# Last batch's end: the last gated product in two token sets, every output tile its own transfer, the last tile in two column halves, and the order of the end drawn anew

## The chip, the cores and the metric

The kernel runs on one core of one Trainium2 chip. The core has a matrix engine (PE in the profile, with its weight loads as PEld), a vector engine (DVE), a scalar engine (ACT), GpSimd (POOL), and SyncE (SP), which here only issues transfers; 16 DMA engines move data between memory and the core. The metric is device time in microseconds, the median of several runs. "About 1%" is what a measurement of it can tell from no change.

## The reference

Clustered attention (4 batches, 8 heads, 768 tokens, head size 64: a query sees only keys whose nearest of 16 centroids is its own), and on its output a gated long convolution.

```python
def _moe_ref(x, w_proj, filter_fft, w_out):      # x: (4, 768, 512), the attention's output
    proj = x @ w_proj
    x1, x2, x3 = (proj[..., :D], proj[..., D:2 * D], proj[..., 2 * D:])
    X2 = np.fft.rfft(x2, n=S, axis=1)
    H = np.fft.rfft(filter_fft, n=S, axis=0)[None, :, :]
    x2_conv = np.fft.irfft(X2 * H, n=S, axis=1)
    y = x1 * x2_conv * x3
    return (y @ w_out).astype(np.float32)
```

All inputs and the output are float32; the output is 4 x 768 x 512.

## The kernel before

`build` makes a plan: a list of operations, each with the engines that could do it, a duration, what it reads and writes, and a due time. `Plan.follow` then lays the operations out in an order written by hand into the string `ORDER`. A word such as `P1543:2` is operation 1543 on PE with its result in PSUM bank 2; V is DVE, A is ACT, G is POOL, S is the SP queue. Each engine does its words from left to right. There are eight PSUM banks (0 to 7; 4 and 5 serve as one pair while attention runs), so a word that takes a bank waits until the last reader of that bank's former content is done.

`attention(n, pr)` does two head pairs at a time, `hyena(b)` does the convolution of batch b. The convolution of batch 2 and the attention of batch 3 are woven together; after them comes the convolution of batch 3, the last, with the rest of batch 2's.

The operations that matter here, by number (up to 1941 the same before and after):

- 1806, 1814, 1822, 1830: the last products of probabilities and values. 1831: the last accumulation of probabilities (L691). 1833: their sum over keys (L704, the denominator), 1834 its copy, 1835 a transpose, 1836 the reciprocal (V), 1837 and 1838 ("bc") spread it over the partitions, 1839 to 1842 multiply and write `xT`, the convolution's input (L772). 1781 and 1782 do the same for the pair before, with `rb`, which S1779 and S1780 load.
- 1843 to 1865: batch 3's projection x2 (1843/1844, 1846/1847, 1850/1851, 1853/1854 each in three quarters, which don't need the last pair, and one; 1857 and 1859 whole), the copies 1845, 1852, 1858, sums and differences on DVE (1848, 1849, 1855, 1856, 1860, 1861) and four sums `uv` (1862 to 1865, L467). 1866 to 1889: the spectrum, times the filter (L833), subtracted or added into `y` (L837: 1872, 1873, 1880, 1881, 1888, 1889).
- For each of four channel blocks dt: projections for x3 and x1 (two halves ch of 384 tokens each, 8 matmuls of 384 columns), a copy of x3 and the gate x1*x3 on DVE (L875), the inverse transform (1899, 1912, 1925, 1938, on two banks), a copy of one bank (1900, 1913, 1926, 1939), two folds (L910, batch 2 also L900), and the gated product `y2[:, dt]` (L913: 1903, 1916, 1929, 1942). For dt = 3: 1930, 1932 (ch 0), 1934, 1936 (ch 1), gates 1933 and 1937, folds 1940 and 1941.
- 1943 to 1964 before: the output. Six tiles of 128 tokens (index 2*tt + e_), each a product over four blocks with `w_out`, three quarters first (needing 1903, 1916, 1929) and one last quarter (needing 1942), then a copy (DVE or ACT) and a transfer on SP: tiles 0 and 1 together (524 KB), 2 and 3 together, 4 and 5 each alone (262 KB).
- Of batch 2: 1496 a projection and 1497 its gate; 1504, 1505, 1519, 1520, 1534, 1535, 1549, 1550 (L900) and 1506, 1507, 1521, 1522, 1536, 1537, 1551, 1552 (L910) its folds; 1508, 1523, 1538, 1553 its gated products; 1524 to 1547 its projections and inverse transforms (1517, 1532, 1547), with the copies 1533, 1544, 1548; 1554, 1556, 1559, 1561, 1564, 1566 its six output tiles, 1560 one of their copies. S1110 is the last 524 KB of batch 1's output.

An operation with `lock=True` on POOL waits for the locked DVE operation ahead of it in the order (L1175 to L1180); DVE doesn't wait for POOL in that way.

PE's products run as pairs of matmuls over 64 columns of weights each (`product`, L65); a product of eight matmuls is one output tile of 128 rows.

Of the kernel before, what the change touches and what calls it, by code (L numbers as in the profile page):

```python
# [23 lines left out]
NT = S // 128  # L24
# [190 lines left out]
A1817 A1811 P1103:1 P1108:3 A1109 P1496:2 V1721 S1779 A1890 S1780 P1502:60 A1503 V1815 V1823 A1104 P1806 P1517:31  # L215
V1505 S1105 A1827 P1511:7 V1831 P1814 P1822 V1504 A1518 P1830 V1512 A1832 V1507 V1506 V1519 V1520 P1833:6 A1834
P1532:07 P1835:6 P1528:5 V1836 P1837:6 V1781 P1838:3 V1782 P1843:1 P1853:4 V1839 V1840 V1841 V1842 P1844 V1497 V1508
P1857:3 A1858 V1522 V1521 G1523 A1533 V1535 P1846:2 V1534 G1536 G1537 A1845 P1847 P1850:6 P1851 V1849 V1848 A1852
P1854 P1859:1 V1860 V1861 P1908:7 A1909 P1547:30 A1529 V1855 V1863 P1539:2 G1862 P1541:7 V1856 G1865 G1864 V1548 V1549
P1524:5 A1525 P1526:1 V1527 A1540 V1542 P1530:6 P1910:2 V1911 V1531 G1538 P1545:5 P1921:1 V1550 G1551 P1866:2 V1867  # L220
P1543:6 A1544 P1869:3 V1868 V1871 V1870 V1546 P1917:0 P1906:2 V1552 A1922 V1553 P1934:1 A1935 P1936:3 V1937 G1872
A1918 P1904:5 G1873 P1919:0 V1920 P1874:1 V1875 P1885:3 P1877:6 P1893:0 V1878 P1556:7 G1880 V1876 V1879 P1882:4 V1883
V1886 A1905 S1110 P1891:5 A1892 G1881 V1884 P1559:1 G1888 P1554:5 P1923:6 P1561:4 A1555 A1557 V1887 V1889 P1895:7
A1896 V1907 V1560 A1562 V1894 P1912:53 V1913 V1914 V1915 P1897:1 V1898 P1899:04 A1900 V1924 S1558 P1564:5 A1565 V1902
P1566:1 A1567 V1901 V1903 P1925:36 A1926 V1916 P1930:1 A1931 P1938:04 S1563 V1927 P1932:1 V1928 V1929 P1957:6 S1568
A1939 V1941 V1940 V1933 V1942 P1953:3 P1950:4 P1943:1 P1958 V1959 S1960 P1951 A1952 P1954 A1955 S1956 P1944 P1946:0
P1947 V1945 A1948 S1949 P1961:4 P1962 A1963 S1964
# [3 lines left out]
def build(T):  # L231
# [548 lines left out]
    def hyena(b):  # L780
# [63 lines left out]
        for dt in range(ND):  # L844
# [58 lines left out]
            for s_, o_ in ((0, Alu.add), (1, Alu.subtract)):  # L903
# [9 lines left out]
            op(("DVE", .95) if last else {"DVE": .95, "POOL": 1.85}, lambda e, dt=dt, x3=x3, yy=yy: alu(e).tensor_tensor(  # L913
                T.y2[:, dt], yy().rearrange("p t c -> p (t c)"), x3().rearrange("p a b -> p (a b)"),
                op=Alu.mult), due + 2.5, r=ykeys + xkeys[0] + xkeys[1], w=[("y2", dt)], lock=True)
        for tt in range(3):
            ob, obk = (T_("tm", 0), [("tm", 0, 0), ("tm", 0, 1), ("tm", 0)]) if last and tt == 2 else (
                T_("ob", tt % 2), [("ob", tt % 2, 0), ("ob", tt % 2, 1), ("ob", tt % 2)])
            for e_ in range(2):
                h = Bank()  # L920
                due = step(.87)

                def W(e, kts=range(ND), tt=tt, e_=e_, h=h):
                    for kt in kts:
                        columns(ap(h), T.y2[:, kt, ts(2 * tt + e_, 128)], T.wout[:, kt], kt == 0, kt == ND - 1)
                if last:
                    op(("PE", .647), lambda e, W=W: W(e, range(3)), due, r=[("y2", dt) for dt in range(3)] + ["wout"],
                       w=[h], alloc=h, kind="proj")
                    op(("PE", .217), lambda e, W=W: W(e, range(3, 4)), due, r=[("y2", 3), h], w=[h], kind="proj")
                else:  # L930
                    op(("PE", .862), W, due, r=[("y2", dt) for dt in range(ND)] + ["wout"], w=[h], alloc=h,
                       kind="proj")
                op(EV512, lambda e, e_=e_, ob=ob, h=h: copy(e, ob()[:, e_], ap(h)), due + 1, r=[h],
                   w=[obk[e_], obk[2]], free=[h])
                if last and tt == 2:
                    op(("SP", .6), lambda e, tt=tt, e_=e_, ob=ob: T.nc.sync.dma_start(
# [274 lines left out]
```

## Time and profile before

| what | us |
|---|---|
| median of three runs | 357.91 (356.87, 357.91, 360.74) |
| the profiled execution | 357.62 |
| its span, first to last instruction | 355.9 |
| its last matmul ends (timeline) | 350.59 |
| its last copy ends (timeline) | 351.27 |

In the lines shown below, a time in front is microseconds from the start of the span; a second number is how long the group lasted. "L913" is line 913 of the kernel, "bank<-wout,y" what is written and read, "x8" how many instructions. In a group "| 3.7, 1826 |" is busy time in us and the mean of one instruction in ns. A bracket tells the engine's idle time before the group and what ended it. Matmuls overlap, and their ends are modelled, so for PE the distance from start to start tells more than the busy time.

### The profile page before, as it was taken

How to read it: one execution, taken by the hardware profiler on the slowest of the kernel's cores; microseconds unless marked ns; L12 is line 12 of the kernel's file. 1: busy time of each engine (PE TensorE's matmuls, PEld its weight loads, DVE VectorE, ACT ScalarE, POOL GpSimd, SP SyncE). 2: the span in 40 equal slices, each digit the busy share in tenths (PEclk: the TensorE clock that was granted, in tenths of full speed). 3: DMA queues.
4: the chain of work that ended last, by engine and by line, in shares of the span. 5: the costliest groups of instructions: out<-in, count | busy, mean ns of one | idle time of the engine just before them, and what ended most of it. 6: DMA issues, size and time to landing. Idle time of an engine off the chain costs nothing.

```text
span 355.9 us, 8355 instructions
## 1 busy us (share of the span) xinstructions
PE 342.5 (96%) x3180; PEld 228.3 (64%) x3180; DVE 330.8 (93%) x444; ACT 274.1 (77%) x511; POOL 160.0 (45%) x181
## 2 busy tenths in 40 slices
PE   6889999999999999999999999999999999999994
PEld 3445454455768577767877457766777857667781
DVE  6899999999999899999998999989999999999892
ACT  4999999999998899778887798889876866133232
POOL 7467134234214846184508737382417272047600
PEclk9899999999999999999999999999999999999999
DMA  9999597796598998789397849782657422400134
GB/s 167 174 198 226 101 149 113 137 200 109 78 181 135 151 153 130 128 129 159 80 203 140 163 83 201 103 166 31 155 91 142 95 82 55 165 2 0 61 122 177
DMA packets 115268, 45.69 MB, mean 128 GB/s; under 512 B 102792, under 2 KB 107420, under 8 KB 115228
## 3 DMA queue, kind: packets, MB, share of 16 engines
q1 hardware_dynamic: 110556, 34.97, 48.4%
q0 software_dynamic: 2960, 9.77, 18.8%
q10 hardware_dynamic: 1712, 0.43, 0.6%
q8 instruction: 25, 0.41, 0.5%
q14 instruction: 15, 0.12, 0.2%
HBM read 31.59 MB, written 7.40 MB: 110 GB/s over the span
## 4 chain that ended last, share of the span: by engine, by line
PE 71%; DVE 11%; ACT 6%; issue 4%; POOL 3%; DMA 3%; SPq 0%; ACTq 0%; DVEq 0%; POOLq 0%
PE bank L70 34%; PE pair L670 26%; PE bank L809 4%; DVE acc L691 2%; ACT p L659 2%; PE bank L588 2%; DMA qkraw<-in_q_dram 2%; ACT p L656 1%; PE bank L477 1%; DMA acc<-acc 1%; ACT aug L248 1%; DVE aug L533 1%; POOL acc L687 1%; PE bank L704 1%; DVE sim L593 1%
## 5 line engine op out<-in xcount | busy, mean ns | idle before, releaser
L670 PE MATMUL pair<-p,vraw 128*64 128x385 f32 x768 | 141.9, 487 | 0.1
L659 ACT ACTIVATE p<-bank 128x512 f32<-128x512 f32 x192 | 107.6, 604 | 20.7 <-PE bank L70 18.5
L691 DVE TENSOR_TENSOR acc<-p,acc 128x1536 f32<-128x1536 f32 x64 | 113.0, 1765 | 2.9 <-ACT p L656 0.6
L70 PE MATMUL bank<-aug 80*64 80x512 bf16 (+3 forms) x738 | 92.4, 330 | 1.3 <-DVE aug L533 0.5
L670 PEld LDWEIGHTS pair<-p,vraw 128*64 128x64 f32 x768 | 68.0, 137 | 35.1 <-issue 18.6
L70 PEld LDWEIGHTS <-aug 128*64 128x64 bf16 (+1 forms) x738 | 66.6, 153 | 33.0 <-issue 22.1
L687 POOL TENSOR_TENSOR acc<-p,p 128x512 f32<-128x512 f32 x35 | 45.6, 1314 | 38.5 <-DVE acc L691 16.0
L656 ACT ACTIVATE p<-bank 128x512 f32<-128x512 f32 x96 | 55.5, 602 | 6.9 <-PE bank L70 6.2
L724 POOL DMA_DIRECT2D acc<-acc x30 | 24.0, 807 | 74.6 <-DMA acc<-acc 38.4
L70 PE MATMUL bank<-xT,wpj 128*64 128x384 bf16 x504 | 49.7, 326 | 0.4 <-ACT p L656 0.4
L248 ACT CAST aug<-qkP 64x768 bf16<-64x768 f32 x51 | 42.2, 829 | 0.9
L70 PEld LDWEIGHTS <-wpj 128*64 128x64 bf16 x504 | 35.1, 110 | 9.0 <-issue 1.4
L70 PEld LDWEIGHTS <-y 128*64 128x64 bf16 x512 | 27.7, 110 | 9.2 <-issue 1.2
L833 DVE TENSOR_TENSOR tm<-bank,hm 128x512 f32<-128x512 f32 x44 | 28.1, 680 | 2.3 <-POOL uv L467 1.2
L837 POOL TENSOR_TENSOR y<-tm 128x512 bf16<-128x512 f32 x17 | 22.2, 1352 | 5.5 <-DVE acc L691 3.1
L913 POOL TENSOR_TENSOR y<-yy,x 128x768 bf16<-128x768 f32 x8 | 14.6, 1830 | 20.4 <-DVE yy L910 18.1
L70 PE MATMUL bank<-wout,y 128*64 128x512 bf16 x192 | 23.8, 379 | 0.0
L809 PE MATMUL bank<-wpj,xT 128*64 128x512 bf16 x192 | 22.4, 379 | 0.0
L559 DVE STREAM_TRANSPOSE qkP<-qkraw 128x768 f32<-128x768 f32 x24 | 22.3, 952 | 0.0
L248 ACT COPY ob<-bank 128x512 f32<-128x512 f32 x20 | 11.6, 590 | 9.6 <-PE bank L70 9.4
L809 PEld LDWEIGHTS <-xT 128*64 128x64 bf16 x192 | 14.6, 110 | 5.3
L772 DVE SCALAR_TENSOR_TENSOR xT<-osb,rb 128x384 bf16<-128x384 f32 x30 | 17.6, 608 | 0.3 <-DMA rb<-dr 0.3
(158 smaller groups left out, 417.4 us busy)
## 6 DMA issues: line engine op xcount, KB each, us to landing
vraw<-in_v_dram SPq DMA_DIRECT2D x16, 384.0 KB
rb<-dr SPq DMA_DIRECT2D x30, 192.0 KB
out_dram<-ob SPq DMA_DIRECT2D x11, 512.0 KB
qkraw<-in_k_dram SPq DMA_DIRECT2D x48, 96.0 KB
qkraw<-in_q_dram SPq DMA_DIRECT2D x48, 96.0 KB
acc<-acc POOLq DMA_DIRECT2D x10, 384.0 KB, 5.3
acc<-acc POOLq DMA_DIRECT2D x10, 192.0 KB, 4.4
wpj<-in_moe_w_proj_dram POOLq DMA_DIRECT2D x4, 384.0 KB, 5.7
```

Of the source, the lines that this page charges most:

```text
L70: T.nc.tensor.matmul(out[64 * i:64 * i + 64], lhsT[:, 64 * i:64 * i + 64], rhs, start=start, stop=stop)
L248: T.nc.scalar.copy(out, in_)
L559: op(("DVE", .9), lambda e, s=s, j=j, pr=pr: V().transpose(T.qkP[pr][:, S * j:S * j + S], T.qkraw[s][:].rearrange("p t h d -> p (t h d)")) ...
L656: T.nc.scalar.activation(o, ap(h).rearrange("p (a b) -> p a b", a=2), Act.Exp, scale=0.125)
L659: T.nc.scalar.activation(flat(s)[:, lo:lo + 512], ap(h), Act.Exp, scale=0.125)
L670: T.nc.tensor.matmul(o[64 * hp:64 * hp + 64, ch, :385], T.vraw[vs][:, hp, sk * D:(sk + 1) * D], T.p[slots[sk]][:, hp, 384 * ch:384 * ch + ...
L687: alu(e).tensor_tensor(o, x, y, op=Alu.add)
L691: T.nc.vector.tensor_tensor(T.acc[os], T.p[slots[sk]][:, :, :S], T.acc[os], op=Alu.add)
L724: op(("POOL", .8), lambda e, rows=rows: T.nc.gpsimd.dma_start(flat_()[:rows], flat_()[rows:2 * rows], accum_op=Alu.add), te, r=[], w=AK, b ...
L809: T.nc.tensor.matmul(ap(h)[64 * i:64 * i + 64], T.xT[xs][:, kt, tokens(m, i, w_)], T.wpj[:, kt, DM:2 * DM], start=kt == 0, stop=kt == ND - 1)
L833: op(("DVE", .68), lambda e, i=i, cs=cs, r=r, h=h: T.nc.vector.tensor_tensor(T.tm[r][:, cs], ap(h), hmrow(i, (0, 2, 2, 3)[2 * r + cs]), op ...
L837: op({"POOL": 1.3, "DVE": .68}, lambda e, i=i, r=r: alu(e).tensor_tensor(T.y[:, i, r], T.tm[r][:, 0], T.tm[r][:, 1], op=Alu.add if r else ...
```

## The change

The last gated product of batch 3 (dt = 3) is cut into two token sets: set 0 is tokens 0 to 191 and 384 to 575, which need the gate of ch 0 and the first fold only; set 1 is the rest. Output tiles 0 and 3 read set 0 alone, tiles 2 and 5 set 1 alone, tiles 1 and 4 both. Every output tile has its own transfer, on SP or ACT. Tile 5 is made in two column halves, each with product, copy and transfer of its own. The end of the order is written anew from batch 1's last output on.

New numbers: 1942 and 1943 are the halves of the product. Tile 0: 1944 (three quarters), 1945 (last quarter), 1946 copy, 1947 transfer; tile 1: 1948 to 1951; tile 2: 1952 to 1955; tile 3: 1956 to 1959; tile 4: 1960 to 1963; tile 5 left: 1964 to 1967, right: 1968 to 1971.

On another engine than before: 1508, 1553 and 1863 from DVE to POOL; 1551, 1862 and 1872 from POOL to DVE; 1548, 1560 and 1913 from DVE to ACT; 1533, 1544 and 1845 from ACT to DVE.

```diff
--- before.py
+++ after.py
@@ -212,19 +212,19 @@
 V1715 V1716 A1772 P1773:2 A1774 G1477 S1717 S1100 P1478:1 P1101:3 A1102 P1481:2 V1479 V1482 V1480 G1484 V1483 V1485
 P1828:6 P1789:45 A1829 P1489:3 P1804:1 G1798 P1824:0 P1486:6 V1487 P1818:2 V1490 A1821 V1488 P1500:7 V1501 A1825 G1492
 V1491 S1775 P1106:0 A1107 V1493 A1819 A1805 V1807 S1718 S1719 V1720 S1776 V1777 S1778 P1796 P1826:7 P1810:2 P1816:0
-A1817 A1811 P1103:1 P1108:3 A1109 P1496:2 V1721 S1779 A1890 S1780 P1502:60 A1503 V1815 V1823 A1104 P1806 P1517:31
-V1505 S1105 A1827 P1511:7 V1831 P1814 P1822 V1504 A1518 P1830 V1512 A1832 V1507 V1506 V1519 V1520 P1833:6 A1834
-P1532:07 P1835:6 P1528:5 V1836 P1837:6 V1781 P1838:3 V1782 P1843:1 P1853:4 V1839 V1840 V1841 V1842 P1844 V1497 V1508
-P1857:3 A1858 V1522 V1521 G1523 A1533 V1535 P1846:2 V1534 G1536 G1537 A1845 P1847 P1850:6 P1851 V1849 V1848 A1852
-P1854 P1859:1 V1860 V1861 P1908:7 A1909 P1547:30 A1529 V1855 V1863 P1539:2 G1862 P1541:7 V1856 G1865 G1864 V1548 V1549
-P1524:5 A1525 P1526:1 V1527 A1540 V1542 P1530:6 P1910:2 V1911 V1531 G1538 P1545:5 P1921:1 V1550 G1551 P1866:2 V1867
-P1543:6 A1544 P1869:3 V1868 V1871 V1870 V1546 P1917:0 P1906:2 V1552 A1922 V1553 P1934:1 A1935 P1936:3 V1937 G1872
-A1918 P1904:5 G1873 P1919:0 V1920 P1874:1 V1875 P1885:3 P1877:6 P1893:0 V1878 P1556:7 G1880 V1876 V1879 P1882:4 V1883
-V1886 A1905 S1110 P1891:5 A1892 G1881 V1884 P1559:1 G1888 P1554:5 P1923:6 P1561:4 A1555 A1557 V1887 V1889 P1895:7
-A1896 V1907 V1560 A1562 V1894 P1912:53 V1913 V1914 V1915 P1897:1 V1898 P1899:04 A1900 V1924 S1558 P1564:5 A1565 V1902
-P1566:1 A1567 V1901 V1903 P1925:36 A1926 V1916 P1930:1 A1931 P1938:04 S1563 V1927 P1932:1 V1928 V1929 P1957:6 S1568
-A1939 V1941 V1940 V1933 V1942 P1953:3 P1950:4 P1943:1 P1958 V1959 S1960 P1951 A1952 P1954 A1955 S1956 P1944 P1946:0
-P1947 V1945 A1948 S1949 P1961:4 P1962 A1963 S1964
+A1817 A1811 P1103:1 P1108:3 A1109 S1110 P1496:2 V1721 S1779 A1890 S1780 P1502:60 A1503 V1815 V1823 A1104 P1806
+P1517:31 V1497 V1505 S1105 A1827 P1511:7 V1831 P1814 P1822 V1504 A1518 P1830 V1512 A1832 P1543:2 V1507 V1506 P1528:6
+P1532:07 V1781 V1782 V1519 V1520 V1533 P1833:5 A1834 P1530:4 P1835:5 V1836 G1508 A1529 P1850:3 P1837:5 V1521 V1522
+P1838:6 V1839 V1840 V1841 V1842 P1843:1 P1846:5 P1844 P1847 V1534 G1523 V1535 V1845 V1848 G1537 P1857:6 A1858 P1859:7
+P1851 P1853:6 G1536 P1854 V1849 A1852 V1860 P1908:5 V1861 V1855 V1862 V1531 V1856 G1863 G1864 P1547:13 A1548 V1544
+V1550 G1865 P1539:7 P1524:0 P1541:4 A1540 V1542 P1526:6 V1549 P1866:2 P1904:7 A1525 V1527 P1891:4 G1538 P1545:6 A1905
+V1867 V1546 P1869:7 V1870 A1909 P1910:5 V1911 V1872 A1892 P1893:6 V1894 V1551 P1934:4 V1552 V1868 G1553 P1895:5
+P1877:3 A1896 P1919:6 P1874:5 P1917:1 A1918 P1885:2 A1935 V1871 G1873 V1875 V1878 G1880 P1897:7 V1898 V1876 V1879
+P1559:1 A1560 P1882:4 G1881 V1883 V1886 V1884 V1887 P1566:7 P1554:1 P1556:3 A1555 G1888 V1889 P1561:5 P1906:4 V1907
+V1920 P1936:2 V1937 A1557 S1558 P1912:13 A1913 V1915 V1914 P1899:62 A1900 V1901 V1902 P1564:4 V1916 A1565 A1562 A1567
+P1925:13 A1926 V1903 V1928 P1921:6 A1922 P1923:7 V1924 V1927 V1929 P1938:25 A1939 V1940 S1563 P1930:7 A1931 S1568
+P1932:3 V1933 V1942 P1952:1 P1964:7 P1944:3 P1945 A1946 P1948:6 V1941 V1943 S1947 P1965 A1966 P1953 A1954 P1968:3
+P1969 A1955 V1970 A1971 P1949 P1956:7 P1957 S1967 V1950 S1951 V1958 S1959 P1960:3 P1961 A1962 A1963
 """
 
 
@@ -910,33 +910,47 @@
                     alu(e).tensor_tensor(o[:, ::-1, :191:-1] if s_ else o[:, :, :192], x[0], x[1], op=o_)
                 op(("DVE", .55) if last else {"DVE": .55, "POOL": 1.02}, fold, due + 2, r=[hh] + okeys if last else skeys, w=ykeys[s_::2], lock=not last,
                    free=[hh] if last else [])
-            op(("DVE", .95) if last else {"DVE": .95, "POOL": 1.85}, lambda e, dt=dt, x3=x3, yy=yy: alu(e).tensor_tensor(
-                T.y2[:, dt], yy().rearrange("p t c -> p (t c)"), x3().rearrange("p a b -> p (a b)"),
-                op=Alu.mult), due + 2.5, r=ykeys + xkeys[0] + xkeys[1], w=[("y2", dt)], lock=True)
+            if last and dt == ND - 1:
+                for g in range(2):
+                    def end(e, g=g, dt=dt, x3=x3, yy=yy):
+                        cut = lambda x: x.rearrange("p (w c) -> p w c", w=2)[:, :, 192 * g:192 * g + 192]
+                        T.nc.vector.tensor_tensor(cut(T.y2[:, dt]), cut(yy().rearrange("p t c -> p (t c)")),
+                                                  x3()[:, :, 192 * g:192 * g + 192], op=Alu.mult)
+                    op(("DVE", .5), end, due + 2.5, r=ykeys[g::2] + xkeys[g] + [("y2", dt)] * g,
+                       w=[("y2", dt, g)] + [("y2", dt)] * (1 - g), lock=True)
+            else:
+                op(("DVE", .95) if last else {"DVE": .95, "POOL": 1.85}, lambda e, dt=dt, x3=x3, yy=yy: alu(e).tensor_tensor(
+                    T.y2[:, dt], yy().rearrange("p t c -> p (t c)"), x3().rearrange("p a b -> p (a b)"),
+                    op=Alu.mult), due + 2.5, r=ykeys + xkeys[0] + xkeys[1], w=[("y2", dt)], lock=True)
         for tt in range(3):
             ob, obk = (T_("tm", 0), [("tm", 0, 0), ("tm", 0, 1), ("tm", 0)]) if last and tt == 2 else (
                 T_("ob", tt % 2), [("ob", tt % 2, 0), ("ob", tt % 2, 1), ("ob", tt % 2)])
-            for e_ in range(2):
+            for e_, c0, c1 in [(0, 0, 512), (1, 0, 512)] if not (last and tt == 2) else [(0, 0, 512), (1, 0, 256), (1, 256, 512)]:
                 h = Bank()
-                due = step(.87)
-
-                def W(e, kts=range(ND), tt=tt, e_=e_, h=h):
+                part = (c1 - c0) / 512
+                due = step(.87 * part)
+
+                def W(e, kts=range(ND), tt=tt, e_=e_, c0=c0, c1=c1, h=h):
                     for kt in kts:
-                        columns(ap(h), T.y2[:, kt, ts(2 * tt + e_, 128)], T.wout[:, kt], kt == 0, kt == ND - 1)
+                        columns(ap(h)[:, :c1 - c0], T.y2[:, kt, ts(2 * tt + e_, 128)], T.wout[:, kt, c0:c1], kt == 0, kt == ND - 1)
                 if last:
-                    op(("PE", .647), lambda e, W=W: W(e, range(3)), due, r=[("y2", dt) for dt in range(3)] + ["wout"],
+                    op(("PE", .647 * part), lambda e, W=W: W(e, range(3)), due, r=[("y2", dt) for dt in range(3)] + ["wout"],
                        w=[h], alloc=h, kind="proj")
-                    op(("PE", .217), lambda e, W=W: W(e, range(3, 4)), due, r=[("y2", 3), h], w=[h], kind="proj")
+                    op(("PE", .217 * part), lambda e, W=W: W(e, range(3, 4)), due,
+                       r=[("y2", 3, g) for g in ((0,), (0, 1), (1,))[(2 * tt + e_) % 3]] + [h], w=[h], kind="proj")
                 else:
                     op(("PE", .862), W, due, r=[("y2", dt) for dt in range(ND)] + ["wout"], w=[h], alloc=h,
                        kind="proj")
-                op(EV512, lambda e, e_=e_, ob=ob, h=h: copy(e, ob()[:, e_], ap(h)), due + 1, r=[h],
-                   w=[obk[e_], obk[2]], free=[h])
-                if last and tt == 2:
-                    op(("SP", .6), lambda e, tt=tt, e_=e_, ob=ob: T.nc.sync.dma_start(
-                        T.out[b].rearrange("(t p) m -> p t m", t=NT)[:, 2 * tt + e_], ob()[:, e_]), due + 2,
-                       r=[obk[e_]], byts=262e3)
-            if not (last and tt == 2):
+                okey = obk[e_] if part == 1 else (obk[e_], c0)
+                op(EV512 if part == 1 else {"ACT": .385, "DVE": .41}, lambda e, e_=e_, c0=c0, c1=c1, ob=ob, h=h: copy(
+                    e, ob()[:, e_, c0:c1], ap(h)[:, :c1 - c0]), due + 1, r=[h],
+                   w=[okey, obk[2]] if part == 1 else [okey], free=[h],
+                   after=() if part == 1 else set(P.writers.get(obk[e_], ())) | set(P.reads.get(obk[e_], ())))
+                if last:
+                    op({"SP": .6, "ACT": .6}, lambda e, tt=tt, e_=e_, c0=c0, c1=c1, ob=ob: dma(e)(
+                        T.out[b].rearrange("(t p) m -> p t m", t=NT)[:, 2 * tt + e_, c0:c1], ob()[:, e_, c0:c1]), due + 2,
+                       r=[okey], byts=262e3 if part == 1 else 132e3)
+            if not last:
                 op(("SP", .7), lambda e, tt=tt, ob=ob: T.nc.sync.dma_start(
                     T.out[b].rearrange("(t p) m -> p t m", t=NT)[:, 2 * tt:2 * tt + 2], ob()), due + 2,
                    r=obk, byts=524e3)
```

## The prediction

> **What bounds the kernel now.** I read the page first, then the chain of work that ended last, then busy time by windows over the last 50 us, then the timeline there. The span is 355.9 us, the profiled execution 357.62 us (1.72 around the span), the median of the runs 357.91, 0.29 above it.
>
> ```profile
> span 355.9 us, 8355 instructions
> ```
> ```profile
> 331.88 18.73 PE bank L70 x264
> ...
> 350.69 0.58 ACT tm L248
> ```
> ```profile
> 311.35:350.60 39.25, 39.24 (x500) 27.73 (x496) 35.60 (x62) 13.13 (x27) 16.65 (x13) 1.00 0.13 48
> 310.90:347.80 36.90, 36.90 (x484) 26.91 (x480) 34.74 (x61) 11.47 (x24) 16.65 (x13) 1.00 0.12 44
> ```
> In the windows the columns are PE, PEld, DVE, ACT, POOL, then clock, DMA share and GB/s. PE is the chain up to its last matmul at 350.59. "Busy" alone would not prove that, since ends are modelled, so I look at starts:
>
> ```profile
> 324.56 4.08 PE L70 MATMUL bank<-xT,wpj 128*64 128x384 bf16 x48
> 328.46 0.61 PE L70 MATMUL bank<-uv,fw 128*64 128x512 bf16 x4
> 332.35 1.91 PE L70 MATMUL bank<-wout,y 128*64 128x512 bf16 x16
> 334.07 0.83 PE L70 MATMUL bank<-xT,wpj 128*64 128x384 bf16 x8
> ```
> From start to start a 384-column matmul takes (328.46-324.56)/48 = 0.081 us and a 512-column one (334.07-332.35)/16 = 0.108; a product of eight is then 0.65 or 0.86. These spacings return throughout the stretch: PE has no hole there that a new order could fill. The last matmul can move little; 5.3 us lie behind it:
>
> ```profile
> 349.05 0.35 SPq L936 DMA_DIRECT2D out_dram<-tm  x1
> 349.57 1.22 SPq L940 DMA_DIRECT2D out_dram<-ob  x2
> 351.30 0.34 SPq L936 DMA_DIRECT2D out_dram<-tm  x1
> ```
> ```profile
> 349.00:350.00 1.00, 1.00 (x14) 0.49 (x12) 0.62 (x2) 0.73 (x3) 0.00 (x0) 1.00 0.10 37
> 350.00:351.00 1.00, 0.59 (x6) 0.11 (x2) 0.00 (x0) 0.71 (x2) 0.00 (x0) 1.00 1.01 371
> 351.00:352.00 1.00, 0.00 (x0) 0.00 (x0) 0.00 (x0) 0.27 (x1) 0.00 (x0) 1.00 1.03 379
> 352.00:353.00 1.00, 0.00 (x0) 0.00 (x0) 0.00 (x0) 0.00 (x0) 0.00 (x0) 1.00 1.02 383
> 353.00:354.00 1.00, 0.00 (x0) 0.00 (x0) 0.00 (x0) 0.00 (x0) 0.00 (x0) 1.00 1.02 381
> 354.00:355.00 1.00, 0.00 (x0) 0.00 (x0) 0.00 (x0) 0.00 (x0) 0.00 (x0) 1.00 0.07 23
> ```
> This is what matters most. The DMA engines run full from about 349.90 to 354.07 and move 37+371+379+383+381+23 = 1574 KB: the last batch's six output tiles of 262 KB, 0.69 us each at 380 GB/s. A transfer issued at 349.05 moves first bytes at 349.90, 0.85 later. The last one, issued at 351.30, alone would end at 351.30+0.85+0.69 = 352.84; it ends at 354.07 because 1.2 us of earlier tiles lie ahead of it. So the end is bound by when this stream begins. From its end to the end of the span are 1.83 us, which stay.
>
> **The change, part by part.**
>
> *Where the stream begins.* All six tiles wait for the last gated product, one 0.96 us instruction. What follows it:
>
> ```profile
> 345.19 5.40 PE L70 MATMUL bank<-wout,y 128*64 128x512 bf16 x48
> 346.21 0.55 DVE L875 TENSOR_TENSOR qkP<-bank,qkP 128x384 f32<-128x384 f32 x1
> 346.80 0.96 DVE L913 TENSOR_TENSOR y<-sim,qkP 128x768 bf16<-128x768 f32 x1
> 348.33 0.69 DVE L250 COPY tm<-bank 128x512 f32<-128x512 f32 x1 [0.57 <-PE bank L70]
> 348.48 1.07 ACT L248 COPY ob<-bank 128x512 f32<-128x512 f32 x2 [3.23 <-PE bank L70]
> ```
> In the new order P1945 completes tile 0, needing the product of the first token set alone (V1942). Behind it PE has, in 512-column matmuls: P1948 6, P1965 1, P1953 2, P1968 3, P1969 1, P1949 2, P1956 6, P1957 2, P1960 6, P1961 2 = 31, times 0.108 = 3.36 us. With the last matmul ending at 350.59, P1945 ends at 347.23. A copy starts 0.10 behind its matmul (350.59 to 350.69) and takes 0.585, its transfer is issued 0.03 later. So:
> tile 0: copied by 347.92, issued 347.95, moves from 348.80 to 349.49.
> tile 5, left columns: matmul done 347.99, copied by 348.5, moves 349.49 to 349.84.
> tile 2: done 348.2, copied on ACT by 349.1, moves 349.97 to 350.66.
> tile 5, right columns: 350.66 to 351.01. tile 1: 351.01 to 351.70. tile 3: copied by 350.5, issued 350.56, 351.70 to 352.39.
> tile 4, last on PE and whole: 350.69+0.585, issued 351.30, could move from 352.15, moves 352.39 to 353.08.
> The stream starts 1.1 earlier, has one gap of 0.13, and ends at 353.08 instead of 354.07: 1.0 us gained. A copy of 256 columns stands in no row; 0.55 for 384 columns (the gate, as long) and 0.69 for 512 differ by 0.14 for 128, so I take 0.41, at worst the whole 0.69. Issues on ACT show only from the start:
>
> ```profile
> 1.24 0.67 ACTq L293 DMA_DIRECT2D qkraw<-in_k_dram  x1
> ```
> Such a transfer has 256-byte pieces, ours 1 and 2 KB as the SP ones, so I take SP's 0.35, at worst 0.67. Both at their worst make the gaps 0.3 us longer: gain 0.7. The gain is at most 1.2, where tile 4's own transfer sets the end (352.84). The tile cut in columns isn't the last one: P1960/P1961 are, so nothing of the 0.585 copy and the 262 KB behind the last matmul shrinks. The halved products cost PE nothing (the same columns, 31 matmuls as counted); a fixed price per matmul would be seen in the narrowest row, 12 of 192 columns:
>
> ```profile
> 338.21 0.68 PE L70 MATMUL bank<-inv,y 128*64 128x192 bf16 x12
> 338.70 0.35 PE L70 MATMUL bank<-qkraw,y 128*64 128x192 bf16 x4
> ```
> (338.70-338.21)/12 = 0.041, in proportion to columns; so zero, at worst 0.1.
>
> The Trainium skill (DMA: Bandwidth & Descriptors, section Bandwidth) gives the rule to batch transfers to 1 MiB or more to reach 75% of peak, which speaks against seven transfers in place of four. By it I would forecast a slower stream. The windows show 371 to 383 GB/s with pieces of 262 and 524 KB queued behind each other, so I do not follow it; as a rival it stands below.
>
> *Does the last matmul stay at 350.59?* The DVE must have the second half (V1943) ready for P1965, which starts (31-6) x 0.108 = 2.70 before PE's end, at 347.88; V1942 for P1945 at 347.01. Locally: from P1932's end PE does P1952, P1964, P1944, 0.65+0.32+0.65 = 1.62, while DVE does gate V1933 (0.55) and V1942 (0.5): about 1.3 with hand-overs. V1941 and V1943 add 1.0, PE adds 0.87. So 0.2 to 0.3 us of slack each. Over the whole stretch: DVE was busy 34.74 of the 36.90 us from its first xT product (310.90) to its last gated product. Out of this go gate 1497 (0.55) and folds 1521, 1522 (1.03), moved ahead; products 1508, 1553 (1.92) to POOL; copies 1548, 1913 (1.10) and 1560 (0.68) to ACT. In come 1544, 1551 (1.10), 1845 (0.68), 1872 (0.69), and 0.05 for the cut: 31.98 us. It now starts 1.86 later (next part): 347.88-312.76 = 35.1 us of room. DVE may idle 3.1; it idled 2.16. So it fits, without much to spare.
>
> *The order ahead of it.* The denominator of the last pair is a chain over three engines:
>
> ```profile
> 307.30 0.85 PE L704 MATMUL bank<-acc,ones 128*32 128x384 f32 x8
> 308.08 0.85 PE L70 MATMUL bank<-inv,y 128*64 128x192 bf16 x16
> 308.22 0.49 ACT L710 ACTIVATE den<-bank 128x384 f32<-128x384 f32 x1
> 308.87 0.55 PE L753 MATMUL bank<-ident,den 128*128 128x128 f32 x3
> 309.25 0.81 PE L68 MATMUL bank<-xT,wpj 128*128 128x384 bf16 x4
> 309.51 0.23 DVE L756 RECIPROCAL dn<-bank 128x12 f32<-128x12 f32 x1 [0.17 <-issue]
> 309.99 1.53 PE L762 MATMUL bank<-ident,dn 128*64 128x128 f32 x24
> 310.92 1.39 DVE L772 SCALAR_TENSOR_TENSOR xT<-osb,bank 128x192 bf16<-128x192 f32 x4 [0.16 <-PE bank L762]
> ```
> Before, 1532 and 1528 filled it: 0.79 for 1532 (308.08 to 308.87) where 16 x 0.041 are 0.66, and 0.74 for 1528 (309.25 to 309.99) where a product needs 0.65, so 0.2 lost. Now 1543, 1528, 1532 run ahead of P1833, 1530 (0.65) beside its eviction, 1850 (0.65) beside the reciprocal: again 0.2 lost. P1837 comes three products of 0.65, less 0.09, later: 1.86. PE's sum is unchanged. On DVE nine operations of about 0.5 lie between the last accumulation and V1836, and gate 1497 ahead:
>
> ```profile
> 304.60 1.75 DVE L691 TENSOR_TENSOR acc<-p,acc 128x1536 f32<-128x1536 f32 x1
> 307.20 1.02 DVE L910 TENSOR_TENSOR yy<-sd 128x384 f32<-128x384 f32 x2
> 301.88 1.12 SPq L742 DMA_DIRECT2D rb<-dr  x2
> ```
> 304.60+1.75+0.46+9 x 0.5 = 311.3, and V1836 is due at 309.51+1.86 = 311.37: no slack. At 0.55 each it comes 0.4 late, and so does PE. S1110 (524 KB, 1.4 us) goes ahead of S1779 and S1780, which land some 1.5 us later, about 306.5; V1781 wants them near 308.8. Without that cover DVE, and then PE, would lose up to 1.4.
>
> *POOL and ACT.* POOL gains two products and loses a fold and a subtraction: +1.4 on 16.65 busy of 39.25.
>
> ```profile
> L467 POOL TENSOR_TENSOR uv<-tm,tm 128x512 bf16<-128x512 f32 x3 | 3.8, 1286 | 1.0 <-DVE uv L467 1.0
> L913 POOL TENSOR_TENSOR y<-yy,x 128x768 bf16<-128x768 f32 x2 | 3.7, 1826 | 18.1 <-DVE yy L910 18.1
> L910 POOL TENSOR_TENSOR yy<-sd 128x384 f32<-128x384 f32 x3 | 3.0, 1017 | 0.2
> ```
> The nearest need is G1863 for P1866. Behind V1842, which ends 312.31+1.86 = 314.2, POOL does G1523 and two folds, 3.9, until 318.1; DVE does two folds of 0.5 and seven operations of 0.61 up to V1862, until 319.4; G1863 then ends at 320.7. PE reaches P1866 after bc (1.36) and fifteen products and parts of products, 8.46 together: 311.85+9.8 = 321.7. So it's covered by 1.0; without the cover PE would wait up to 1.3. ACT's two issues A1955 and A1971 stand ahead of A1962 and are over by 350. The SP queue holds only S1947, S1967, S1951, S1959 there, none waiting for a later one.
>
> Sum: -1.0 for the stream, +0.1 for the last matmul (bounds -0.2, the old loss at the denominator, to +1.2, from the first rival): 357.91-0.9 = 357.0.
>
> **The rivals.**
> 1. *DVE sets the end.* If its idle time doubles from 2.16 to 4.3, V1943 is 1.2 late and P1965 and all behind it follow one for one. For: slack of 0.2 to 0.3 at several hand-overs, 0.0 at V1836. Against: 1 to 2 us less DVE work. It decides once V1943 ends over 1.0 behind P1965's place; then the kernel is slower than before: 357.91-1.0+1.3 = 358.2.
> 2. *The stream doesn't tighten.* Gaps between smaller pieces and 1 KB rows that cost as much as 2 KB ones (0.35), with ACT's slow issues (0.3) and late copies, leave 0.2 of the 1.0: 357.7. Against: no gap in the rows between pieces.
> 3. *Each transfer pays its start-up alone.* Three more transfers at 0.85 are 2.55: 357.91-1.0+2.55 = 359.5. The windows speak against it: four transfers, one start-up seen. That skill page's rule on batching points this way.
> 4. *More gain*: the waits around the denominator vanish and tile 4 alone sets the end: 357.91-1.4 = 356.5.
>
> **How the numbers follow.** Forecast 0.52 (356.6 to 357.4), rival 1 0.20, rival 2 0.12, rival 3 0.05, rival 4 0.11. A measurement tells about 1%, 3.6 us, from no change: below 354.3 lies no case, since PE's work and the 262 KB behind it stay, so 0.02; above 361.5 only a much worse rival 1, 3 or the lost cover of S1110, 0.06; within, 0.92. Range 355.8 to 358.9: rivals 1, 2 and 4 with 0.7 on either side, as the three runs shown spread from 1.04 below their median.
>
> **What would show it.** Right: DMA windows full from about 348.8, ending near 353.1; last matmul within 0.3 of 350.6; the first output transfer of the end issued near 348 and seven in all; no idle in front of P1965. Wrong: a last matmul past 351, with PE waiting for V1942 or V1943 or bc for the reciprocal; windows under 350 GB/s, or holes in them; a gap between ACT's copy and its own issue.

## The result, and the profile after

The changed kernel takes 356.93 us (median of 17 runs, 355.25 to 360.7), the kernel before 358.62 in the same session (17 runs, 356.87 to 361.32). The ratio is 0.9941, 95% interval 0.9916 to 0.9965: a gain of 0.6%, below the 1% that the forecast took as the bound, and about 2.1 us where 0.9 was forecast. (The ratio is that of the means without one slow run of 360.7 us; the medians lie 1.7 apart.) The runs of one and the same program spread over 5 us, so I needed a reading with less scatter before asking where the time went.

The timeline of PE gives one. Up to the last three value products (the row of 24 matmuls on L670) PE does the same in both programs; the new order moves only one gate (V1497) and one output transfer (S1110) ahead of it. Here is that row in the kernel before, after, and in a second profile of the changed kernel:

```profile
303.29 4.08 PE L670 MATMUL pair<-p,vraw 128*64 128x385 f32 x24
```
```profile
303.89 4.08 PE L670 MATMUL pair<-p,vraw 128*64 128x385 f32 x24
```
```profile
309.75 4.08 PE L670 MATMUL pair<-p,vraw 128*64 128x385 f32 x24
```
The spans are 355.9, 355.4 and 361.2 us (the last at a granted clock of 0.988). From the row's start to the end of the span are 52.61, 51.51 and 51.50 us. I call this the stretch. The changed program's two profiles differ by almost 6 us in span and by 0.02 in the stretch. The change gained 1.1 us there. Times below that stand "behind the row" count from the row's start; those of packets are from the trace's DMA records. The "stream" is what the DMA engines move of the last batch's output, from its first packet to its last.

The end of the changed kernel, first DVE, ACT, the weight loads (PEld) and the queues in the timeline, then busy time by windows:

```profile
346.15 0.55 DVE L875 TENSOR_TENSOR qkP<-bank,qkP 128x384 f32<-128x384 f32 x1
346.73 0.56 DVE L917 TENSOR_TENSOR y<-sim,qkP 128x384 bf16<-128x384 f32 x1
347.21 0.55 DVE L910 TENSOR_TENSOR sim<-bank,rb 128x384 f32<-128x384 f32 x1
347.34 0.63 PEld L70 LDWEIGHTS <-y 128*64 128x64 bf16 x8 [0.24 <-DVE y L917]
347.79 0.56 DVE L917 TENSOR_TENSOR y<-sim,qkP 128x384 bf16<-128x384 f32 x1
347.84 0.58 ACT L248 COPY ob<-bank 128x512 f32<-128x512 f32 x1 [2.04 <-PE bank L70]
348.40 2.41 PEld L70 LDWEIGHTS <-y 128*64 128x64 bf16 x30 [0.43 <-DVE y L917]
348.45 0.35 SPq L950 DMA_DIRECT2D out_dram<-ob  x1
348.80 0.37 ACT L248 COPY tm<-bank 128x256 f32<-128x256 f32 x1 [0.38 <-PE bank L70]
349.07 0.59 ACT L248 COPY ob<-bank 128x512 f32<-128x512 f32 x1
349.20 0.34 SPq L950 DMA_DIRECT2D out_dram<-tm  x1
349.50 0.42 DVE L250 COPY tm<-bank 128x256 f32<-128x256 f32 x1 [1.15 <-PE bank L70]
349.69 0.37 ACTq L950 DMA_DIRECT2D out_dram<-ob  x1
349.84 1.39 DVE L250 COPY ob<-bank 128x512 f32<-128x512 f32 x2
350.11 0.47 ACTq L950 DMA_DIRECT2D out_dram<-tm  x1
350.55 1.04 SPq L950 DMA_DIRECT2D out_dram<-ob  x2
351.34 0.58 ACT L248 COPY tm<-bank 128x512 f32<-128x512 f32 x1 [1.68 <-PE bank L70]
351.96 0.34 ACTq L950 DMA_DIRECT2D out_dram<-tm  x1
```
```profile
349.00:350.00 1.00, 1.00 (x16) 0.67 (x12) 0.50 (x2) 0.66 (x2) 0.00 (x0) 1.00 0.69 254
350.00:351.00 1.00, 1.00 (x13) 0.45 (x8) 0.98 (x2) 0.00 (x0) 0.00 (x0) 1.00 0.84 291
351.00:352.00 1.00, 0.30 (x4) 0.00 (x0) 0.23 (x1) 0.58 (x1) 0.00 (x0) 1.00 1.02 361
352.00:353.00 1.00, 0.00 (x0) 0.00 (x0) 0.00 (x0) 0.00 (x0) 0.00 (x0) 1.00 1.04 391
353.00:354.00 1.00, 0.00 (x0) 0.00 (x0) 0.00 (x0) 0.00 (x0) 0.00 (x0) 1.00 0.74 277
```
The two halves of the product (L917) take 0.56 each. Tile 0 is copied from 347.84, before the second half is finished, and its transfer is issued at 348.45; the stream runs from 349.30. The matmuls end at 351.30, 47.41 behind the row, where they ended at 47.30 before. The stream ends at 49.97 instead of 50.91. The share of 0.84 in the second window is the hole between the left half of tile 5 and tile 2, whose copy starts on ACT at 349.07, behind the left half's, and whose transfer is issued at 349.69. In the DMA records tile 2's first packet starts at 46.70 behind the row, and from about 46.9 on the engines are busy up to the end.

The denominator's chain, again from the timeline of PE:

```profile
309.86 0.85 PE L704 MATMUL bank<-acc,ones 128*32 128x384 f32 x8
310.64 0.84 PE L70 MATMUL bank<-xT,wpj 128*64 128x384 bf16 x8
311.41 0.55 PE L753 MATMUL bank<-ident,den 128*128 128x128 f32 x3
311.89 0.84 PE L809 MATMUL bank<-wpj,xT 128*64 128x512 bf16 x6
312.56 1.48 PE L762 MATMUL bank<-ident,dn 128*64 128x128 f32 x24
```
From the sum to bc are 312.56-309.86 = 2.70 us, with two other products in between, where it was 2.69 with two others: neutral, as reckoned.

### The profile page after: what moved, and what is told of

Read it like the earlier page. It is cut to its first block, busy times and chain, and to the rows that moved or that the text cites. A ratio compares the mean times of both kernels' runs of the same rounds, so it can differ in the third digit from the quotient of the medians.

```text
span 355.4 us, 8385 instructions
## 1 busy us (share of the span) xinstructions
PE 341.2 (96%) x3189; PEld 224.8 (63%) x3192; DVE 332.6 (94%) x446; ACT 274.0 (77%) x511; POOL 160.4 (45%) x181
## 4 chain that ended last, share of the span: by engine, by line
PE 70%; ACT 9%; DVE 7%; DMA 5%; issue 4%; POOL 4%; SPq 1%; ACTq 0%; DVEq 0%; POOLq 0%
PE bank L70 34%; PE pair L670 26%; PE bank L809 4%; ACT p L659 2%; PE bank L588 2%; DVE acc L691 2%; ACT aug L248 2%; DMA rb<-dr 2%; DMA qkraw<-in_q_dram 2%; PE bank L477 1%; ACT p L656 1%; DMA acc<-acc 1%; DVE aug L533 1%; POOL acc L687 1%; POOL uv L467 1%
## 5 line engine op out<-in xcount | busy, mean ns | idle before, releaser
L670 PE MATMUL pair<-p,vraw 128*64 128x385 f32 x768 | 141.6, 487 | 0.1
L670 PEld LDWEIGHTS pair<-p,vraw 128*64 128x64 f32 x768 | 67.1, 137 | 35.8 <-issue 20.5
L70 PEld LDWEIGHTS <-wpj 128*64 128x64 bf16 x512 | 34.2, 109 | 11.3 <-issue 2.3
L922 POOL TENSOR_TENSOR y<-yy,x 128x768 bf16<-128x768 f32 x10 | 18.2, 1824 | 20.7 <-DVE xT L772 15.7
L70 PE MATMUL bank<-wout,y 128*64 128x512 bf16 (+1 forms) x200 | 23.9, 371 | 0.8 <-POOL y L922 0.8
L837 POOL TENSOR_TENSOR y<-tm 128x512 bf16<-128x512 f32 x16 | 20.9, 1353 | 3.2 <-DVE acc L691 2.9
```

What stands on the lines that cost most here:

```text
L70: T.nc.tensor.matmul(out[64 * i:64 * i + 64], lhsT[:, 64 * i:64 * i + 64], rhs, start=start, stop=stop)
L670: T.nc.tensor.matmul(o[64 * hp:64 * hp + 64, ch, :385], T.vraw[vs][:, hp, sk * D:(sk + 1) * D], T.p[slots[sk]][:, hp, 384 * ch:384 * ch + ...
L837: op({"POOL": 1.3, "DVE": .68}, lambda e, i=i, r=r: alu(e).tensor_tensor(T.y[:, i, r], T.tm[r][:, 0], T.tm[r][:, 1], op=Alu.add if r else ...
```

## The experiments

All readings, in us behind the row except the first column (the row's own start):

| kernel | row starts | last matmul | first packet | last packet | stretch |
|---|---|---|---|---|---|
| before | 303.29 | 47.30 | 46.60 | 50.91 | 52.61 |
| after | 303.89 | 47.41 | 45.41 | 49.97 | 51.51 |
| after again | 309.75 | 47.41 | 45.41 | 49.96 | 51.50 |
| whole product | 303.72 | 47.98 | 46.23 | 50.58 | 52.12 |
| paired transfers | 303.09 | 47.41 | 46.15 | 51.12 | 52.75 |
| old order, own transfers | 303.56 | 47.29 | 46.59 | 50.85 | 52.42 |
| two transfers left out | 303.67 | 47.29 | 46.58 | 49.66 | 50.99 |
| halved tile last | 303.06 | 47.68 | 45.40 | 49.97 | 51.54 |
| quarter last | 306.40 | 47.54 | 45.41 | 50.17 | 51.75 |
| end undone | 301.46 | 47.97 | 46.49 | 51.68 | 53.31 |
| halved last, free bank | 305.40 | 47.42 | 45.41 | 49.97 | 51.52 |
| quarter last, free bank | 304.19 | 47.27 | 45.41 | 50.17 | 51.75 |
| three more early | 304.60 | 47.41 | 45.41 | 49.97 | 51.29 |
| three more early, again | 303.43 | 47.41 | 45.40 | 49.97 | 51.29 |

Each reading is of one profile; the two kernels that were profiled twice repeat to 0.02. Times were also taken of the whole product (ratio to the kernel before 0.9986, interval 0.9961 to 1.0011), the paired transfers (0.9991, 0.9972 to 1.001) and the old order with own transfers (0.9993, 0.997 to 1.0015). They can't be told from the kernel before, nor from the changed kernel's second timing below: what the experiments show, they show in the stretch.

**The changed kernel again**, no edit.

> The changed kernel once more, unaltered. I read the stretch from the first matmul of the last three value products (the row of 24 on L670) to the end of the span: before it is 355.9-303.29 = 52.61 us, after 355.4-303.89 = 51.51. Theory (all of the gain lies in this stretch, the rest of the measured difference is scatter of the first 303 us, where both programs do the same): the stretch is 51.5 +-0.15 again, the start of the row lies anywhere from 302 to 306, and the ratio is 0.997 within its interval. Rival (the changed program also runs its first 303 us faster): ratio 0.994 again and the row starts about 1 us earlier than in the kernel before.

Stretch 51.50; ratio 0.9987, interval 0.9962 to 1.0011, against 0.9941 at first. The theory holds as to the stretch; the row's start, 309.75, is outside the 302 to 306 that were expected. Over all fourteen profiles it lies from 301.46 to 309.75, and the two profiles of the changed kernel alone are 5.86 apart. The largest part of this scatter can be read in the traces. At about 236 us DVE goes from fold to fold in the changed kernel's first profile; in the second it waits there for a product on POOL:

```profile
DVE yy L910 <- POOL y L922: 3.7, 1, 3.7
```
The same wait is 3.8 us in "halved last, free bank", 2.8 in "quarter last", 1.6 in "three more early", 0.9 in "quarter last, free bank" and 0.4 in "whole product", and the other eight profiles don't have it. The five with 0.9 or more are the five in which the row starts latest. What holds POOL up wasn't followed further.

The run also says what a single time is worth here: "end undone" took 356.53 us in its one time, shorter than all three runs first shown of the kernel before, with the longest stretch of all, 53.31, because its row started at 301.46.

**The product whole again.**

```diff
-                for g in range(2):
-                    def end(e, g=g, dt=dt, x3=x3, yy=yy):
...
+                op(("DVE", .95), lambda e, dt=dt, x3=x3, yy=yy: T.nc.vector.tensor_tensor(
+                    T.y2[:, dt], yy().rearrange("p t c -> p (t c)"), x3().rearrange("p a b -> p (a b)"), op=Alu.mult),
+                   due + 2.5, r=ykeys + xkeys[0] + xkeys[1], w=[("y2", dt), ("y2", dt, 0), ("y2", dt, 1)], lock=True)
...
-P1932:3 V1933 V1942 P1952:1 P1964:7 P1944:3 P1945 A1946 P1948:6 V1941 V1943 S1947 P1965 A1966 P1953 A1954 P1968:3
+P1932:3 V1933 V1942 P1952:1 P1964:7 P1944:3 P1948:6 V1941 V1943 P1945 A1946 S1947 P1965 A1966 P1953 A1954 P1968:3
```

> The changed kernel with the last gated product whole again, at the place of its second half; three quarters of tile 1 go ahead of the last quarter of tile 0 on PE to fill the wait. Theory (the stream of output begins when tile 0 is copied, and that waits for the first half): tile 0 about 0.85 later, of which 0.3 is hidden because the stream had a gap; the stretch is 52.0 to 52.2, the last matmul at most 0.15 later. Rival (the halves don't matter, separate transfers do): 51.5.

Stretch 52.12, within what was expected: the halves are worth 0.6 us. The stream begins 0.82 later. The last matmul is 0.57 later, not 0.15; the timeline of this kernel shows why:

```profile
348.49 0.59 ACT L248 COPY ob<-bank 128x512 f32<-128x512 f32 x1 [2.86 <-PE bank L70]
...
349.13 2.14 PE L70 MATMUL bank<-wout,y 128*64 128x256 bf16 x22 [0.35 <-ACT ob L248]
```
P1968 takes bank 3 from tile 0, so a later tile 0 holds back PE as well: 0.35 us by the modelled ends, 0.52 by the starts of the single matmuls. I had counted the product and not the bank behind it.

**Transfers paired again.**

```diff
+                if last and tt < 2:
+                    op({"SP": .6, "ACT": .6}, (lambda e: None) if not e_ else lambda e, tt=tt, ob=ob: dma(e)(
+                        T.out[b].rearrange("(t p) m -> p t m", t=NT)[:, 2 * tt:2 * tt + 2], ob()), due + 2,
+                       r=obk[:2] if e_ else [], byts=524e3)
-                if last:
+                elif last:
```

> The changed kernel with tiles 0 and 1, and 2 and 3, each in one transfer again, sets and order kept. Theory (the start of the stream sets the end): the first large transfer waits for tile 1's copy, about 2 us later than tile 0's; the left half of tile 5 starts earlier but is only 0.35 of stream; stretch 52.6 to 53.0. Rival (fewer transfers run faster, or the end is set by tile 4's own chain): 51.3 to 51.6.

Stretch 52.75 with the last matmul unmoved at 47.41: own transfers are worth 1.2 us in the new order. The stream begins with the left half of tile 5 at 46.15; by the DMA records the next pieces begin at 46.93 (the right half) and 47.54 (tiles 0 and 1), with a hole in front of each.

**Own transfers in the old order.**

```diff
-                op(EV512, lambda e, e_=e_, ob=ob, h=h: copy(e, ob()[:, e_], ap(h)), due + 1, r=[h],
-                   w=[obk[e_], obk[2]], free=[h])
+                def out(e, tt=tt, e_=e_, ob=ob, h=h):
+                    copy(e, ob()[:, e_], ap(h))
+                    if last and tt < 2:
+                        T.nc.sync.dma_start(T.out[b].rearrange("(t p) m -> p t m", t=NT)[:, 2 * tt + e_], ob()[:, e_])
+                op(EV512, out, due + 1, r=[h], w=[obk[e_], obk[2]], free=[h])
...
-                op(("SP", .7), lambda e, tt=tt, ob=ob: T.nc.sync.dma_start(
+                op(("SP", .7), (lambda e: None) if last else lambda e, tt=tt, ob=ob: T.nc.sync.dma_start(
```

> The kernel before, order kept, but every output tile of the last batch its own transfer on SP, issued behind its copy. Theory (the stream is bandwidth-bound and its first piece, tile 4, starts at the same time): stretch 52.6 +-0.1 as before. Rival 3 of the prediction (each transfer pays 0.85 of its own): two more transfers, 54.3. Rival (separate transfers alone give the gain): 51.5.

The stream runs from 46.59 to 50.85, as before with 46.60 to 50.91. Its windows are as full with 262 KB pieces:

```profile
351.00:352.00 1.00, 0.00 (x0) 0.00 (x0) 0.00 (x0) 0.53 (x1) 0.00 (x0) 1.00 1.03 385
352.00:353.00 1.00, 0.00 (x0) 0.00 (x0) 0.00 (x0) 0.00 (x0) 0.00 (x0) 1.00 1.03 379
353.00:354.00 1.00, 0.00 (x0) 0.00 (x0) 0.00 (x0) 0.00 (x0) 0.00 (x0) 1.00 1.01 383
```
Rival 3 (a start-up for each transfer) falls, and so does the idea that smaller transfers alone gain. Yet the stretch is 52.42, just under the 52.5 expected and 0.19 shorter than before, of which only 0.06 lie in the stream. The rest is behind the last packet; see the ring below.

**Two transfers left out**, in the kernel before.

```diff
-                op(("SP", .7), lambda e, tt=tt, ob=ob: T.nc.sync.dma_start(
+                op(("SP", .7), (lambda e: None) if last else lambda e, tt=tt, ob=ob: T.nc.sync.dma_start(
```

> The kernel before without the two 524 KB transfers of the last batch's tiles 0 to 3 (that part of the output is not written). Theory (the end is the end of a full stream, 1.2 us of which stand in front of the last tile): the last tile moves 0.85 behind its issue and the last packet lands 1.2 earlier than before, 49.7 us behind the first value product of the row on L670 instead of 50.91; the stretch is 51.2 to 51.4. Rival (the last transfer's own start-up and landing set the end): last packet at 50.9, stretch 52.6.

The last packet lands at 49.66, 1.25 earlier, with the last matmul unmoved: the last tile did wait behind a full stream. Its windows show tile 4, nothing, and the last tile alone:

```profile
350.00:351.00 1.00, 0.96 (x10) 0.27 (x6) 0.00 (x0) 0.59 (x1) 0.00 (x0) 1.00 0.69 260
351.00:352.00 1.00, 0.00 (x0) 0.00 (x0) 0.00 (x0) 0.59 (x1) 0.00 (x0) 1.00 0.01 2
352.00:353.00 1.00, 0.00 (x0) 0.00 (x0) 0.00 (x0) 0.00 (x0) 0.00 (x0) 1.00 0.48 182
353.00:354.00 1.00, 0.00 (x0) 0.00 (x0) 0.00 (x0) 0.00 (x0) 0.00 (x0) 1.00 0.22 80
```
Its stretch of 50.99 is 0.2 below what I expected, again behind the last packet.

**The halved tile truly last**, and a variant with only its last quarter there.

```diff
-P1932:3 V1933 V1942 P1952:1 P1964:7 P1944:3 P1945 A1946 P1948:6 V1941 V1943 S1947 P1965 A1966 P1953 A1954 P1968:3
-P1969 A1955 V1970 A1971 P1949 P1956:7 P1957 S1967 V1950 S1951 V1958 S1959 P1960:3 P1961 A1962 A1963
+P1932:3 V1933 V1942 P1952:1 P1964:7 P1944:3 P1945 A1946 P1948:6 V1941 V1943 S1947 P1965 A1966 P1953 A1954
+A1955 P1949 S1967 V1950 S1951 P1956:7 P1957 V1958 S1959 P1960:3 P1961 A1962 A1963 P1968:1 P1969 V1970 S1971
```
The variant puts `P1968:4` in front of `P1965` and leaves `P1969 V1970 S1971` at the end.

> The changed kernel with the right half of tile 5 as the last work of PE, behind tile 4, its transfer on SP. Theory (stream first, then the last piece's chain): tiles 1, 3 and 4 come 0.4 earlier on PE, the last piece is 131 KB with a copy of 0.42; the last packet lands at 49.7 behind the first value product of the row instead of 49.98, the stretch is 51.2 to 51.3 against 51.52. Rival (the end is bound by the stream alone, which begins at the same time): 51.5.

> As the run with the halved tile last, but three quarters of that right half run early, in bank 4, in the 0.15 us in which PE waits for the second half product; only its last quarter (two matmuls) comes behind tile 4. Theory: the last matmul ends at 47.25 instead of 47.41 behind the first value product of the row, the last packet at 49.55 to 49.65, the stretch is 51.1 to 51.2; the ratio to the kernel before is 0.996 within 0.0025. Rival (stream alone): 51.5.

Both missed: 51.54 and 51.75 (the second timed: 0.999, interval 0.9968 to 1.0013). PE lost 0.26 us in front of tile 3's product: it takes bank 7 from the left half of tile 5, and the work that had covered that copy was the work I had moved away. So I gave tile 3 the free bank 0 (`P1956:0`) in both:

> The run with the halved tile last, with tile 3's product in bank 0, which is free, instead of bank 7, whose copy it waited 0.26 us for. Theory (the two orders lost to a bank, the rest of the reckoning holds): last matmul at 47.4 behind the first value product of the row instead of 47.68, last packet at 49.7 to 49.8, stretch 51.25 to 51.35. Rival (a stream that begins at 45.4 ends at 49.97 whatever comes last): 51.5.

> The run with only the last quarter of the halved tile behind tile 4, with tile 3's product in bank 0. Theory: last matmul at 47.27 instead of 47.54, last packet at 49.75 to 49.9 (the left half of tile 5 stays 0.2 late), stretch 51.3 to 51.45. Rival: 51.7 as with bank 7.

The matmuls came to 47.42 and 47.27 as reckoned, and the last packet didn't follow: 49.97 and 50.17, to 0.01 as with bank 7. So the theory missed once more and the rivals held: the last piece's own chain isn't what binds; the stream is. In the first, the queues issue the last piece at 353.40, 48.0 behind the row, early enough to move by 48.9:

```profile
349.96 0.35 SPq L950 DMA_DIRECT2D out_dram<-ob  x1
350.71 0.34 SPq L950 DMA_DIRECT2D out_dram<-tm  x1
351.20 0.37 ACTq L950 DMA_DIRECT2D out_dram<-ob  x1
351.41 1.20 SPq L950 DMA_DIRECT2D out_dram<-ob  x2
353.03 0.35 ACTq L950 DMA_DIRECT2D out_dram<-tm  x1
353.40 0.33 SPq L950 DMA_DIRECT2D out_dram<-tm  x1
```
The DMA records say more than the rival did, which went by the first packet at 45.41. In the changed kernel and in this order the engines have work without a hole only from the third piece on, tile 2, whose first packet starts at 46.70 in both; the end follows 3.27 us later in both. The variant delays the second and the third piece by some 0.17 us: tile 2 starts at 46.87 and the end follows 3.30 later, 0.2 later than in the changed kernel, although the first packet is the same and PE is done earlier.

**The end undone**: whole product and paired transfers together (both diffs above), the new order and the column halves kept.

> The changed kernel with whole last product and tiles 0 and 1, 2 and 3 paired in one transfer: the new order and the column halves alone. Theory (losses of the two add, since each delays the start of the stream): stretch 53.0 to 53.4, slower than the 52.61 before, with the last matmul at 48.0 as with the whole product alone. Rival (the new order itself carries the gain): 51.5 to 52.1.

Stretch 53.31, as expected. The new order and the column halves bring nothing by themselves; without the early start of the stream they are 0.7 worse than the old order: its matmuls end 0.67 later, and its stream has only half a tile at the head (46.49) and then holes. The column halves were not tried alone, nor the halved product in the old order, so what either is worth without the rest is not shown.

**The ring.** At the end of the program SP checks a row of semaphores (the counters that tell it that a transfer has landed). To move the last transfer's place in that row, three output transfers of the first batch are cut in two, long before the end (the profile has them between 198 and 270 us, so the "200 us before the end" of the expectation is really 158 to 86):

```diff
-                op(("SP", .7), lambda e, tt=tt, ob=ob: T.nc.sync.dma_start(
-                    T.out[b].rearrange("(t p) m -> p t m", t=NT)[:, 2 * tt:2 * tt + 2], ob()), due + 2,
-                   r=obk, byts=524e3)
+                op(("SP", .7), lambda e, tt=tt, ob=ob: [T.nc.sync.dma_start(
+                    T.out[b].rearrange("(t p) m -> p t m", t=NT)[:, 2 * tt + i:2 * tt + i + n], ob()[:, i:i + n])
+                    for i, n in ([(0, 1), (1, 1)] if b == 0 else [(0, 2)])], due + 2, r=obk, byts=524e3)
```

> The changed kernel with the first batch's three output transfers cut into two each, 200 us before the end: three more transfers in the program. Behind the last packet the span goes on for 1.70, 1.63, 1.57, 1.55 us with 4, 5, 6, 7 transfers at the end and 1.33 with 2. Theory (SP checks the transfers' semaphores one after another at 0.06 us, in a fixed ring, and the place of the last transfer in the ring counts): ten more or two is the same place in a ring of eight, so 1.33 here, last matmul and last packet unchanged at 47.41 and 49.97, stretch 51.3. Rival (the length depends on the size or on the number of transfers in flight at the end): 1.55, stretch 51.5.

Last matmul and last packet didn't move, and the span ends 1.32 us behind the last packet instead of 1.54: stretch 51.29. Timed in a further run:

> The run with three more early transfers once more, timed: of all runs it has the shortest stretch. Theory: stretch 51.3 +-0.03 (1.3 less than before, 0.2 less than the changed kernel), and a ratio of 1-1.3/358 = 0.996 within an interval of about +-0.0025, which can't tell it from the changed kernel's 0.997. Rival (the place in the ring is drawn anew in each execution): stretch anywhere from 51.2 to 51.7.

51.29 again, ratio 0.9941 (interval 0.991 to 0.9971). It is the shortest stretch of any version that writes the whole output, 0.22 below the changed kernel; the times can't tell the two apart.

## Why the prediction was right, and where it was off

- *The end is bound by the start of a full DMA stream*: right, shown by leaving out two transfers (the last packet 1.25 earlier, 1.2 reckoned) and by the two orders in which tiles 1, 3 and 4 came earlier from PE and the end did not. In the changed kernel, though, it isn't the first piece that binds but the third, behind the hole.
- *The stream starts 1.1 and ends 1.0 earlier*: it starts 1.19 and ends 0.94 earlier. The first packet was reckoned at 348.80-303.29 = 45.51 behind the row and came at 45.41, the last at 49.79 and came at 49.97. Of these 0.18 us, 0.13 are a misreading of the kernel before, whose last packet landed at 354.20 and not at 354.07. The stream lasts 4.56 us where it lasted 4.31, so 0.25 longer where a gap of 0.13 was reckoned: the window with the hole is 0.16 short of full, the DMA records show a smaller gap (0.06) between tile 0 and the left half of tile 5, and the packets' own time adds up to 0.06 more on each engine.
- *The last matmul +0.1*: it was +0.11. But it did not belong in the sum: the last matmul wasn't what the end waited for. The DVE reckoning held too. From its first xT product to the second half product the windows show, in the changed kernel:

```profile
313.48:348.35 34.87, 34.87 (x464) 23.86 (x458) 32.17 (x58) 11.78 (x24) 16.13 (x12) 1.00 0.13 47
```
32.17 us of work where 31.98 was reckoned, and 2.7 of idling where 3.1 were free. What little it lacked is the 0.15 us that PE waited for V1943 before P1965 (weight load at 348.40, above). Rival 1 was at work, at a tenth of its price. The output moved ahead of the loads of `rb` cost nothing: V1781 follows the fold in front of it without a gap, in the timeline of DVE:

```profile
308.72 0.55 DVE L910 TENSOR_TENSOR yy<-sd 128x384 f32<-128x384 f32 x1
309.19 1.14 DVE L772 SCALAR_TENSOR_TENSOR xT<-osb,rb 128x384 bf16<-128x384 f32 x2
```
- *From its end to the end of the span are 1.83 us, which stay*: this step failed. By packets they were 1.70, and they shrank by 0.16, to 1.54. Before, SP waited once, long, for the last transfer, and then checked the rest; after, it had checked several while the stream ran. The views of what SP waited for, before and after:

```profile
SPq L1206 <- DMA out_dram<-tm: 2.8, 1, 2.8
```
```profile
SPq L1220 <- DMA out_dram<-ob: 1.3, 2, 0.7
...
SPq L1220 <- DMA out_dram<-tm: 1.2, 2, 0.7
```
So the stretch lost 0.94 in the stream, in which the later matmuls are contained, and 0.16 behind it: 1.10, where -1.0+0.1 = -0.9 was forecast. That is close, but two of the three terms are off: the 0.16 was not foreseen, and the 0.1 was added for nothing.
- *Rival 2* (gaps and slow issues on ACT): the issue took 0.34 to 0.47 us, a 1 KB row 47 ns against 86 for 2 KB; of its 0.8 us came the 0.12 by which the stream grew more than reckoned. Its worst case was added up too low: 0.28 for a slow copy and 0.32 for a slow issue stand one behind the other in front of tile 2, so the gaps could have been 0.6 longer and not 0.3, and the gain 0.4 and not 0.7. As the copy of 256 columns took 0.37, nothing hung on it. *The rule on batching to 1 MiB* that the Trainium skill (DMA: Bandwidth & Descriptors, section Bandwidth) gives isn't borne out here: 262 KB pieces queued behind each other run at 379 to 385 GB/s.
- The first ratio, 0.9941, is a gain of 2.1 us, 1.0 more than the stretch has; the second, 0.9987, is 0.6 less, and its interval holds 1. The stretch is the same in both. That the first median, 356.93, lies beside the 357.0 of the forecast is luck: the forecast started from 357.91, the median of three runs, and seventeen gave 358.62. Of the several us by which the first 303 us of one program vary, up to 3.8 are DVE's wait for POOL at about 236 us; what makes that wait come and go stays open, as does whether a part of the 0.9941 lies in the first 303 us.

## What to carry to other kernels

When the last thing a kernel does is write its output, see first whether the DMA engines are full up to the end. Where they were, in this kernel, neither an earlier last matmul nor a smaller last piece helped; what counted was the moment from which the stream ran without a hole, and small pieces that started early beat large ones as long as the next piece was ready in time. Where an unchanged beginning scatters by more than the change can bring, read the changed stretch from a common row of the trace; it repeated to 0.02 us. When work moves in an order with few banks, look at what it had been covering: four of the versions tried lost 0.26 to 0.52 us to a bank that a copy still held.

## What was not expected of the hardware

Behind the last packet the span goes on for a time that depends on the place of the last transfer among the checks that SP makes at the end (L1206 before, L1220 after), one after another, at about 0.06 us each. With 2, 4, 5 and 6 transfers at the end it was 1.33, 1.70, 1.63 and 1.57 us, with 7 from 1.54 to 1.58; with 7 and three more early in the program 1.32, twice. The trace's semaphore records show why. The transfers take eight semaphores in turn (numbers 100, 102 to 106, 108 and 109), and SP always checks them in this order. The transfer that lands last had 100 in the kernel before, the first, so seven more checks followed; in the changed kernel it had 104, the fourth; with three more early transfers, and with two left out, it had 108, the seventh. Three more transfers early in the program thus brought its end 0.22 us forward without any later transfer moving, and over all versions the difference is 0.4 us.
